# Softmax of head pairs reordered, V products ahead of scores, one K read in halves

## The chip, the cores and the metric

The kernel runs on one core of a Trainium2 chip. Its engines each run their own instruction stream in order: TensorE (PE in the profile, its weight loads PEld), VectorE (DVE), ScalarE (ACT), GpSimd (POOL) and SyncE (SP), which here only issues DMAs. The metric is the device time of one execution in microseconds (us); the median of three runs before the change is 1168.55.

## The reference

Eight tokens of width 512 go through two layers of the same shape. Each layer is grouped-query attention with a cache, and then a small dense block, each with layer norm ahead of it and a residual behind it:

```python
def _A_ref(x, k_cache, v_cache, wq, wo):
    q = (x @ wq).reshape(B, 1, 32, 128)          # 32 query heads
    k = jnp.repeat(k_cache, 4, axis=1)           # 8 K/V heads, 8192 keys each
    v = jnp.repeat(v_cache, 4, axis=1)
    p = softmax(einsum("bhqd,bhkd->bhqk", q, k) * 128 ** -0.5)
    return einsum("bhqk,bhkd->bhqd", p, v).reshape(B, 1, 4096) @ wo

x = x + _A_ref(layernorm(x), ...)
x = x + silu(layernorm(x) @ w1) @ w2
# ... and both lines once more, with the same caches and weights
```

Everything is bf16. K and V of one batch entry and one head are 2 MB each, 128 MB for each cache. Both layers read the same caches, but layer 2 of a batch entry can only begin when its layer 1 is done.

## The kernel before, in words

**Tasks.** A task is (layer, batch entry, K/V head); there are 2 x 8 x 8 = 128. The code counts layers from 0 and so does this text. `make_tasks` orders them: for each batch entry b, heads 0 to 2 of layer 0, then heads 3 to 7 of layer 0, some filling tasks of other entries, then heads 3 to 7 of layer 1, whose K is still in the memory on the chip ("kept": the last KEEP = 20 of the 32 quarters of K), and later heads 0 to 2 of layer 1, whose K is read again. V is read in both layers.

**Positions.** The main loop (L1105) walks positions p, eight for each task (GPT) and two for each quarter of a head's keys (GPG). At each position it issues, in this order: the transposes of the quarter that comes next (`emit_t_until`), the scores of the quarter just complete (`emit_s`), the product of probabilities and V of the quarter that lies LP = 22 positions back (`emit_pv`), the steps that finish a head, `emit_own`, `emit_join` and `emit_fold`, one phase of the softmax of the task two back (`softmax`, phase p % 8), a step of the dense block, the normalisation (`emit_norm`), and the reads whose place has come (`issue_until`). Since each engine takes its instructions in order, this order is the order on every engine.

**A task's work.** K lies in one of 28 slots of 512 KB (a quarter of a head each). VectorE transposes it in place (L516, 1.2 us a quarter). TensorE makes the scores: `emit_s` at L606, or, for kept heads of a pair, `score_both` at L578. Heads 4 and 5, and 6 and 7, are pairs (DUOS): their softmax is made together, with scores in two PSUM banks. The softmax has phases: 0, row maxima and a maximum over the partitions on GpSimd (L620 to L629); 2, the shift and the first exponential on ScalarE (L635 to L642, with the row sums as a by-product); 3, for a pair, the transposition of the first probabilities on TensorE (L667) and the second exponential; 4, the sums scaled by the head mask (L652 on ScalarE for a single head, L655 on VectorE for a pair) and summed over the partitions on GpSimd (L658); 5, the last transposition and the copy to PT (L674); 7, the reciprocal (L681). The probabilities, the joined output and the fold's input all share the tile E, so `emit_own` (L728, ScalarE) must wait for the transpositions, `emit_join` (L736, VectorE) for L728, and the fold (L750, TensorE) for the join. `emit_norm` (L760, VectorE) multiplies by the reciprocal. `emit_pv` (L711) takes two quarters at once for a head of a pair, at even quarters.

**Reads.** `plan_loads` lists every read with the position that needs it, sorts by that, and deals slots: a read's place (`after`) is the position behind which its slot is free, and never earlier than that of the read ahead of it. All reads go through SyncE's queue in this one order, so one read that waits for its slot holds all behind it. A V read of a single head is 512 KB, of a pair's head 1 MB (two slots). Kept K of heads 4 to 7 is read in one piece of 2 MB (READ[g] = 4, four slots); kept K of head 3 too. Slots of V come free behind L711, slots of K that is not kept behind L606 in the same layer, slots of kept K behind the scores of layer 1, which `emit_s` makes for all four quarters at the third one (SCORED = 2).

**Scores of kept heads.** In layer 0 a head whose K came in pieces of READ[g] quarters is scored when a piece's last quarter has been transposed: with READ[7] = 4, at the fourth quarter. The two lines that decide this:

```python
w = NGRAN if layer else READ[g]
if whole and (k != SCORED if layer else k % w != w - 1):
    return
```

Of the kernel before, what the change touches and what calls it, by code (L numbers as in the profile page):

```python
# [19 lines left out]
READ = (1, 1, 1, 4, 4, 4, 4, 4)  # L20
DUOS = (4, 6)
KEEP = 20
LT = 1
# [121 lines left out]
class Load:  # L145


    __slots__ = ("kind", "b", "g", "k", "turn", "need", "free", "slot", "after", "wide")

    def __init__(self, kind, b, g, k, need, free, wide=1):  # L150
        self.kind, self.b, self.g, self.k, self.turn = kind, b, g, k, k
        self.need, self.free, self.wide = need, free, wide
        self.slot, self.after = None, None
# [48 lines left out]
def plan_loads(tasks, kept, nslot, ngran):  # L202

    at = {t: i for i, t in enumerate(tasks)}
    loads = []
    for i, (layer, b, g) in enumerate(tasks):
        for k in range(ngran):
# [8 lines left out]
            w = members(g)  # L216
            if k % w == 0:
                loads.append(Load("V", b, g, k, i0 + GPG - 1 + LP, i0 + GPG - 1 + LP, w))
    loads.sort(key=lambda d: (d.need, d.kind == "K" and d.wide == 1))
# [43 lines left out]
def _build(ctx, nc, A_x, A_k_cache, A_v_cache, A_wq, A_wo, B_w1, B_w2, out):  # L263
# [43 lines left out]
    def half(slot, h):  # L307
# [30 lines left out]
              "top": DR, "tops": DR, "ssm": DR, "xn": KT // 2, "hs": FT // 2}  # L338
    widths.update({f"ssa{n}": DR for n in range(NST)})
# [71 lines left out]
    v_slot = {}  # L411

    def issue(d):
        cache = A_k_cache if d.kind == "K" else A_v_cache
        own, lead, n = d.g - lead_of(d.g), lead_of(d.g), members(d.g)
        if d.kind == "K":
            rows = cache[d.b, lead:lead + n].rearrange("g (p f) d -> (g p) (f d)", p=128 // n)
            at = own if d.wide > 1 else d.k * n + own
            src = rows[:, at * d.wide * SLOT:(at + 1) * d.wide * SLOT]
        else:  # L420
            src = cache[d.b, d.g].rearrange("(k p c) d -> k p (c d)", k=NGRAN // n, p=128)[d.k // n]
# [7 lines left out]
    with nc.Block() as block:  # L429

        @block.sync
        def _(sync_eng):
# [137 lines left out]
            def score_both(ti, slots, qn):  # L570
                own = tasks[ti][2] - lead_of(tasks[ti][2])
                cols = NGRAN // 2 * 128
                many = ARENA[:, slots[0] * SLOT:(slots[0] + NGRAN) * SLOT].rearrange(
                    "p (k u t x h j e) -> p u t h e k x j", u=2, t=NQ, x=CPB, h=PAIRS, e=2, j=QUAD)
                for u in range(2):
# [3 lines left out]
                            SCp[bank][t * QUAD:t * QUAD + USED, own * cols:(own + 1) * cols], QB[qn][:, n, :],  # L579
# [4 lines left out]
            def emit_s(i):  # L584
# [10 lines left out]
                if whole and members(g) > 1:  # L595
                    score_both(ti, slots, qn)
# [51 lines left out]
            def softmax_sum(ti):  # L648
                st, many = turn_of[ti] % NST, members(tasks[ti][2])
                w = many * REP  # L650
                if many == 1:
                    op(act, lambda: act.activation(ssm[:, 0:w], hm[:, :], ACT.Copy, scale=rs[st][:, 0:1]),  # L652
                       reads=["hm", f"rs{st}"], writes=["ssm"])
                else:
                    op(dve, lambda: dve.scalar_tensor_tensor(  # L655
                        ssm[:, 0:w], rs[st][:, 0:1].to_broadcast([128, w]), rs[st][:, 1:2], hm2, op0=ALU.add, op1=ALU.mult),
                       reads=["hm2", f"rs{st}"], writes=["ssm"])
# [43 lines left out]
            def emit_pv(i):  # L701
                ti = i // GPT
                b, g, k, _h = where(i)
                if k % members(g):
                    return
# [486 lines left out]
```

## Time and profile before

| what | value |
| --- | --- |
| runs | 1166.80, 1169.06, 1168.55 us; median 1168.55 |
| profiled execution | 1169.76 us, of which the span from the first to the last instruction is 1168.0 |
| TensorE matmul busy | 692.2 us, 59% of the span |
| VectorE busy | 738.9 us, 63% |
| ScalarE busy | 315.1 us, 27% |
| GpSimd busy | 90.7 us, 8% |
| read from HBM | 465.05 MB, mean 400 GB/s |
| mean granted TensorE clock | 0.616 |

Busy shares are means over stages with different limits. The table of windows splits the span into stretches and gives for each the busy time of every engine, the granted clock, the share of DMA time and the rate; the timeline gives single instructions with the idle time ahead of them in brackets and what ended it; the table of waits sums such idle times by pair. A share of DMA time over 1 means that packets overlap on an engine.

### The profile page before, as it was taken

How to read it: one execution, taken by the hardware profiler on the slowest of the kernel's cores; microseconds unless marked ns; L12 is line 12 of the kernel's file. 1: busy time of each engine (PE TensorE's matmuls, PEld its weight loads, DVE VectorE, ACT ScalarE, POOL GpSimd, SP SyncE). 2: the span in 40 equal slices, each digit the busy share in tenths (PEclk: the TensorE clock that was granted, in tenths of full speed). 3: DMA queues.
4: the chain of work that ended last, by engine and by line, in shares of the span. 5: the costliest groups of instructions: out<-in, count | busy, mean ns of one | idle time of the engine just before them, and what ended most of it. 6: DMA issues, size and time to landing. Idle time of an engine off the chain costs nothing.

```text
span 1168.0 us, 28238 instructions
## 1 busy us (share of the span) xinstructions
PE 692.2 (59%) x11792; PEld 377.8 (32%) x11792; DVE 738.9 (63%) x1719; ACT 315.1 (27%) x700; POOL 90.7 (8%) x232
## 2 busy tenths in 40 slices
PE   1525566556665566466665575456765576466676
PEld 1212343234233243133332342234332343133343
DVE  3836655876387664777477655777467664777473
ACT  0342123222322223312222233213322233312322
POOL 0000010001000010001100010001100010001000
PEclk9855565556655575655666577655565555666665
DMA  9999999999999999999999999999999999999993
GB/s 361 404 401 399 408 402 426 417 389 408 401 419 383 399 407 421 422 373 410 412 422 413 395 407 424 420 387 402 412 423 412 391 405 419 423 393 409 412 411 147
DMA packets 94175, 466.90 MB, mean 400 GB/s; under 512 B 9936, under 2 KB 14048, under 8 KB 71904
## 3 DMA queue, kind: packets, MB, share of 16 engines
q1 hardware_dynamic: 94048, 465.10, 98.8%
q8 instruction: 93, 1.52, 0.5%
q14 instruction: 34, 0.28, 0.1%
HBM read 465.05 MB, written 0.01 MB: 398 GB/s over the span
## 4 chain that ended last, share of the span: by engine, by line
DMA 40%; PE 19%; DVE 17%; issue 12%; ACT 6%; SPq 3%; POOL 2%; DVEq 0%; ACTq 0%; POOLq 0%
DMA arena<-in_A_k_cache_dram 33%; DMA arena<-in_A_v_cache_dram 7%; DVE E L736 6%; PE OTp L711 6%; DVE arena L516 4%; ACT E L642 4%; DVE row L620 3%; PE SCp L578 3%; SPq L394 3%; PE TPp L667 2%; PE SCp L606 2%; PE MISC L855 2%; ACT PT L674 1%; PE MISC L873 1%; PE OTp L750 1%
## 5 line engine op out<-in xcount | busy, mean ns | idle before, releaser
L516 DVE STREAM_TRANSPOSE arena<-arena 128x1024 int32<-128x1024 int32 x352 | 430.1, 1231 | 120.0 <-DMA arena<-in_A_k_cache_dram 119.9
L642 ACT ACTIVATE E<-SCp,row 128x512 bf16<-128x512 f32 x128 | 180.8, 1413 | 538.1 <-DVE row L638 463.5
L711 PE MATMUL OTp<-arena,PT 128*16 128x512 bf16 (+1 forms) x2064 | 259.9, 560 | 50.9 <-DMA arena<-in_A_v_cache_dram 31.0
L736 DVE SCALAR_TENSOR_TENSOR E<-OTp,row,E 128x128 f32<-128x128 f32 x381 | 130.4, 342 | 115.3 <-ACT E L728 97.9
L606 PE MATMUL SCp<-arena,QB 128*16 128x128 bf16 (+1 forms) x3328 | 139.3, 314 | 101.6 <-DVE arena L516 87.0
L667 PE MATMUL TPp<-ident,E 128*128 128x128 bf16 x512 | 73.4, 293 | 121.1 <-ACT E L642 120.5
L578 PE MATMUL SCp<-arena,QB 128*16 128x256 bf16 x2048 | 114.0, 389 | 47.1 <-DVE arena L516 30.4
L606 PEld LDWEIGHTS SCp<-arena,QB 128*16 128x16 bf16 x3328 | 70.3, 110 | 173.5 <-DVE arena L516 138.8
L667 PEld LDWEIGHTS TPp<-ident,E 128*128 128x128 bf16 x512 | 41.6, 125 | 185.9 <-ACT E L642 164.2
L750 PE MATMUL OTp<-row,E 128*128 128x4 f32 x254 | 66.4, 332 | 47.3 <-DVE E L736 46.9
L750 PEld LDWEIGHTS OTp<-row,E 128*128 128x128 f32 x254 | 55.4, 272 | 115.6 <-DVE E L736 103.2
L578 PEld LDWEIGHTS SCp<-arena,QB 128*16 128x16 bf16 x2048 | 61.0, 117 | 97.1 <-DVE arena L516 46.1
L629 POOL PARTITION_ALL_REDUCE row<-row x96 | 36.0, 375 | 689.7 <-DVE row L626 575.1
L728 ACT ACTIVATE E<-OTp,row 128x128 f32<-128x128 f32 x127 | 47.4, 373 | 152.4 <-PE OTp L711 152.4
L620 DVE TENSOR_REDUCE row<-SCp 128x1 f32<-128x512 f32 x128 | 86.3, 674 | 2.8
L711 PEld LDWEIGHTS OTp<-arena,PT 128*16 128x16 bf16 (+1 forms) x2064 | 53.5, 107 | 84.7 <-DMA arena<-in_A_v_cache_dram 40.4
L873 PE MATMUL MISC<-at,wo 128*128 128x32 bf16 x1024 | 37.0, 186 | 56.4 <-DVE at L760 55.3
L674 ACT COPY PT<-TPp 128x256 bf16<-128x256 bf16 x128 | 44.3, 372 | 84.6 <-PE TPp L667 84.6
L658 POOL PARTITION_ALL_REDUCE row<-row x96 | 41.3, 431 | 297.5 <-ACT row L652 137.9
L655 DVE SCALAR_TENSOR_TENSOR row<-row 128x8 f32<-128x8 f32 x32 | 7.3, 229 | 88.7 <-ACT E L642 88.7
L873 PEld LDWEIGHTS MISC<-at,wo 128*128 128x128 bf16 x1024 | 32.6, 104 | 65.9 <-DVE at L760 58.8
L563 DVE TENSOR_TENSOR QB<-QSp,row 128x64 bf16<-128x64 f32 (+1 forms) x128 | 24.0, 194 | 15.7 <-PE QSp L547 14.6
(104 smaller groups left out, 385.5 us busy)
## 6 DMA issues: line engine op xcount, KB each, us to landing
arena<-in_A_v_cache_dram SPq DMA_DIRECT2D x256, 512.0 KB, 8.5
arena<-in_A_v_cache_dram SPq DMA_DIRECT2D x128, 1024.0 KB, 12.2
arena<-in_A_k_cache_dram SPq DMA_DIRECT2D x192, 512.0 KB, 8.1
arena<-in_A_k_cache_dram SPq DMA_DIRECT2D x40, 2048.0 KB, 16.1
wq<-in_A_wq_dram SPq DMA_DIRECT2D x1, 4096.0 KB, 17.3
wo<-in_A_wo_dram SPq DMA_DIRECT2D x1, 4096.0 KB, 33.3
w<-in_B_w_dram SPq DMA_DIRECT2D x2, 1792.0 KB, 24.8
E<-in_A_x_dram SPq DMA_DIRECT2D x1, 8.0 KB
```

The source lines that it names most:

```text
L516: op(dve, lambda: dve.transpose(words, words), reads=[r_half(slot, 0), r_half(slot, 1)], writes=[r_half(slot, 0), r_half(slot, 1)])
L578: lambda n=n, t=t: pe.matmul(SCp[bank][t * QUAD:t * QUAD + USED, own * cols:(own + 1) * cols], QB[qn][:, n, :], many[:, u, t, n // 2, n % ...
L606: lambda n=n, t=t: pe.matmul(SCp[bank][t * QUAD:t * QUAD + USED, lo * 128:(lo + len(slots)) * 128], QB[qn][:, n, :], keys(t, n), start=(n ...
L620: op(dve, lambda: dve.tensor_reduce(rowmax[:, n:n + 1], SCp[bank][:, :], AX.X, ALU.max), reads=[f"SC{bank}"], writes=["rowmax"])
L642: op(act, lambda: act.activation(P[:, :].rearrange("p (x j k) -> p k x j", x=CPB, k=NGRAN), SCp[bank][:, :].rearrange("p (k x j) -> p k x ...
L667: lambda c=c: pe.transpose(tpv[:, c, :], P[:, c * 128:(c + 1) * 128], ident[:, :])
L674: op(act, lambda: act.copy(PT[pb][:, :, :, :, :].rearrange("p a t x r -> p x t a r"), tpv.rearrange("p x (t q) -> p x t q", q=QUAD)[:, :, ...
L711: lambda t=t, y=y, slot=slot, pb=pb: pe.matmul(OTp[ob][t * QUAD:t * QUAD + w * REP, 0:w * DH], PT[pb][:, at, t, y * w:(y + 1) * w].rearran ...
L728: op(act, lambda: act.activation(joint, OTp[ob][:, 0:DH], ACT.Copy, scale=own_x[:, 0:1]), reads=[f"OT{ob}", "own_x"], writes=["P"])
L736: op(dve, lambda x=x: dve.scalar_tensor_tensor(joint, OTp[ob][:, x * DH:(x + 1) * DH], own_x[:, x:x + 1], joint, op0=ALU.mult, op1=ALU.add ...
L750: lambda: pe.matmul(OTp[ob][:, 0:REP], joint, hm[:, :], start=True, stop=True)
L873: lambda o=o, h=h: pe.matmul(MISC[:, o * w:(o + 1) * w], wo_sb[:, h, o * 128:(o + 1) * 128], rhs_of(h).to_broadcast([128, w]) if n == 1 el ...
```

## The change

Six things are changed.

1. READ of head 7 goes from 4 to 2: its kept K is read in two pieces of 1 MB, and in layer 0 `score_both` is called for each half, with the columns that belong to it. In layer 1 it is still called once.
2. At positions where a kept head would be scored, `emit_pv` is issued ahead of `emit_s`.
3. For a pair, phases move: the first transposition and the second exponential from phase 3 to 4, the last transposition and the copy to PT from 5 to 6, the sums from 4 to 7. Phase 6 is issued ahead of `emit_own`, `emit_join` and `emit_fold` of the same position, all other phases behind them as before.
4. For a pair, the two row sums are scaled by the mask in two ScalarE instructions into 16 columns, in place of one on VectorE into 8; GpSimd's sum is over 16 columns; VectorE adds the two halves ahead of the reciprocal.
5. The reciprocal is made in `emit_norm` of the first head of a task or pair instead of phase 7.
6. `plan_loads` gets a loop: V reads of 1 MB with fewer than AMPLE = 8 positions between place and need are cut in two. `emit_pv` follows each read's width.

The diff, cut to its core:

```diff
-READ = (1, 1, 1, 4, 4, 4, 4, 4)
+READ = (1, 1, 1, 4, 4, 4, 4, 2)
+AMPLE = 8
...
 def plan_loads(tasks, kept, nslot, ngran):
+    apart = set()
+    while True:
+        loads = deal(tasks, kept, nslot, ngran, apart)
+        close = {d.key for d in loads if d.kind == "V" and d.wide > 1 and d.need - d.after < AMPLE}
+        if not close:
+            return loads
+        apart |= close
...
-            at = own if d.wide > 1 else d.k * n + own
+            at = (own * NGRAN + d.k) // d.wide if d.wide > 1 else d.k * n + own
...
-            def score_both(ti, slots, qn):
+            def score_both(ti, slots, qn, first):
                 own = tasks[ti][2] - lead_of(tasks[ti][2])
-                cols = NGRAN // 2 * 128
+                lo = (own * NGRAN + first) // 2 * 128
+                hi = lo + len(slots) // 2 * 128
...
             def softmax_sum(ti):
                 st, many = turn_of[ti] % NST, members(tasks[ti][2])
                 w = many * REP
-                if many == 1:
-                    op(act, lambda: act.activation(ssm[:, 0:w], hm[:, :], ACT.Copy, scale=rs[st][:, 0:1]),
-                       reads=["hm", f"rs{st}"], writes=["ssm"])
-                else:
-                    op(dve, lambda: dve.scalar_tensor_tensor(
-                        ssm[:, 0:w], rs[st][:, 0:1].to_broadcast([128, w]), rs[st][:, 1:2], hm2, op0=ALU.add, op1=ALU.mult),
-                       reads=["hm2", f"rs{st}"], writes=["ssm"])
-                op(pool, lambda: pool.partition_all_reduce(ssa[st][:, 0:w], ssm[:, 0:w], 128, bass.bass_isa.ReduceOp.add),
+                for n in range(many):
+                    op(act, lambda: act.activation(ssm[:, n * w:(n + 1) * w], masks[many][0], ACT.Copy, scale=rs[st][:, n:n + 1]),
+                       reads=["hm", "hm2", f"rs{st}"], writes=["ssm"])
+                op(pool, lambda: pool.partition_all_reduce(
+                    ssa[st][:, 0:many * w], ssm[:, 0:many * w], 128, bass.bass_isa.ReduceOp.add),
                    reads=["ssm"], writes=[f"ssa{st}"])
...
             def softmax_rcp(ti):
-                st, w = turn_of[ti] % NST, members(tasks[ti][2]) * REP
+                st, many = turn_of[ti] % NST, members(tasks[ti][2])
+                w = many * REP
+                if many > 1:
+                    op(dve, lambda: dve.tensor_tensor(ssa[st][:, 0:w], ssa[st][:, 0:w], ssa[st][:, w:2 * w], ALU.add),
+                       reads=[f"ssa{st}"], writes=[f"ssa{st}"])
                 op(dve, lambda: dve.reciprocal(ssa[st][:, 0:w], ssa[st][:, 0:w]), reads=[f"ssa{st}"], writes=[f"ssa{st}"])
...
-                elif ph == 3 and many > 1:
+                elif ph == 4 and many > 1:
                     emit_turn(ti, 0)
                     softmax_exp(ti, 1)
                 elif ph == 4:
                     softmax_sum(ti)
-                elif ph == 5:
+                elif ph == 5 and many == 1 or ph == 6 and many > 1:
                     emit_turn(ti, many - 1)
                     emit_pt(ti)
-                elif ph == 7:
-                    softmax_rcp(ti)
+                elif ph == 7 and many > 1:
+                    softmax_sum(ti)
...
             def emit_norm(ti):
                 layer, b, g = tasks[ti]
                 ob, st, own = ti % 2, turn_of[ti] % NST, g - lead_of(g)
+                if not own:
+                    softmax_rcp(ti)
...
-                if p % GPG == GPG - 1 and p < NG:
+                scored = p % GPG == GPG - 1 and p < NG
+                behind = scored and (tasks[p // GPT][2], p % GPT // GPG) in kept
+                if scored and not behind:
                     emit_s(p)
                 if (p - LP) % GPG == GPG - 1 and 0 <= p - LP < NG:
                     emit_pv(p - LP)
+                if behind:
+                    emit_s(p)
+                probs = p // GPT - 2
+                due_now = 0 <= probs < ntask and lead_of(tasks[probs][2]) == tasks[probs][2]
+                if due_now and p % GPT == 6:
+                    softmax(probs, 6)
...
-                ti = p // GPT - 2
-                if 0 <= ti < ntask and lead_of(tasks[ti][2]) == tasks[ti][2]:
-                    softmax(ti, p % GPT)
+                if due_now and p % GPT != 6:
+                    softmax(probs, p % GPT)
```

## The prediction

> **What bounds the kernel now.** First the page: its row of DMA shares and its table of queues.
>
> ```profile
> DMA  9999999999999999999999999999999999999993
> q1 hardware_dynamic: 94048, 465.10, 98.8%
> ```
>
> The transfers are busy in every slice but the last. 465 MB have to come in, the change adds no byte, and the last 19 us (from 1149) hold no pair of heads: they stay. So I ask only where the stream runs below its rate. The table of windows of 10 us, whose last columns are DMA share and GB/s, shows it:
>
> ```profile
> 480.00:490.00 10.00, 4.85 (x57) 2.32 (x56) 8.26 (x19) 2.34 (x5) 0.82 (x2) 0.68 1.01 418
> 500.00:510.00 10.00, 6.20 (x92) 3.14 (x84) 9.33 (x18) 0.37 (x1) 0.00 (x0) 0.67 1.00 376
> 510.00:520.00 10.00, 6.15 (x106) 3.54 (x106) 7.26 (x15) 3.75 (x7) 0.77 (x2) 0.50 0.93 334
> 540.00:550.00 10.00, 6.87 (x163) 4.59 (x164) 7.54 (x21) 3.38 (x12) 1.41 (x4) 0.58 1.02 408
> ```
>
> It runs at 415 to 426 where reads of 1 and 2 MB dominate, at 408 where all are 512 KB, and dips once per batch: 350 at 110, 363 at 240, 349 at 370, 334 at 510, 377 at 640, 356 at 770, 363 at 910, 381 at 1040. Against 415, with the slice beside each, that is 15.8 us in all; no gain at these places can exceed it. The dips come when head 7 of a batch has been scored. What is late there, by the waits:
>
> ```profile
> DVE row L655 <- ACT E L642: 88.7, 32, 3.7
> SPq L107 <- PE OTp L711: 431.4, 152, 7.7
> SPq L394 <- PE SCp L578: 91.0, 19, 9.3
> ```
>
> VectorE stands still 32 times, 2.8 us each, until ScalarE has made the second exponential of a pair; SyncE waits for V products (L711) to free slots. The timeline of one dip (batch 3; x in brackets is the idle time before):
>
> ```profile
> 496.57 0.23 DVE L655 SCALAR_TENSOR_TENSOR row<-row 128x8 f32<-128x8 f32 x1 [2.49 <-ACT E L642]
> 499.68 1.06 PE L711 MATMUL OTp<-arena,PT 128*16 128x512 bf16 x8
> 499.81 1.25 DVE L516 STREAM_TRANSPOSE arena<-arena 128x1024 int32<-128x1024 int32 x1 [1.86 <-DMA arena<-in_A_k_cache_dram]
> 500.84 0.33 SPq L394 DMA_DIRECT2D arena<-in_A_v_cache_dram  x1
> ...
> 506.09 1.25 DVE L516 STREAM_TRANSPOSE arena<-arena 128x1024 int32<-128x1024 int32 x1 [0.35 <-DMA arena<-in_A_k_cache_dram]
> 507.46 1.07 PE L711 MATMUL OTp<-arena,PT 128*16 128x512 bf16 x8
> 508.62 0.33 SPq L394 DMA_DIRECT2D arena<-in_A_v_cache_dram  x1
> 515.44 0.23 DVE L655 SCALAR_TENSOR_TENSOR row<-row 128x8 f32<-128x8 f32 x1 [2.64 <-ACT E L642]
> 522.29 1.25 DVE L516 STREAM_TRANSPOSE arena<-arena 128x1024 int32<-128x1024 int32 x1 [1.94 <-DMA arena<-in_A_k_cache_dram]
> ```
>
> Three L516 wait for landings, and they gauge the stream. From 499.81 (head 7's K) to 506.09 (the next K) lie 2.62 MB: 6.28 us, 417 GB/s, no gap. From 506.09 to 522.29 lie 6.29 MB (three 1 MB reads of V, six 512 KB reads of K): 16.20 us, 388 GB/s. The seven batches that show both waits have a second stretch of 15.67, 16.46, 16.20, 15.58, 15.79, 15.97 and 16.38, mean 16.01. At 416 to 424 GB/s it takes 15.1 to 14.8. So 0.9 to 1.2 us per batch is truly lost; the rest of a dip is engines that ran ahead and wait for the slowest.
>
> **The change, part by part.**
>
> *V products first.* For kept heads L711 is issued ahead of the scores at the same position: layer 0's last quarter, layer 1's third. At 498.00 the scores of head 6 (1.89 us) stood ahead of the product at 499.68; its probabilities were ready at 497.89 (end of the L674 copies), so it can start 1.8 us earlier, and the V read of 500.84 leaves at about 499.1. The product at 507.46 stood behind the scores of head 7 (505.79, which waited for transposes); its V lands about 4.9 us after head 7's K, at 504.7, so the read of 508.62 leaves near 506. These are what the stretch behind 506.09 lacks: with them 4.2 MB not yet landed at 506 are issued by 509, or 10 us of stream, to about 516, and the next V read (513.53, behind the product at 512.37, which nothing here moves) and K read (514.60) come in time. The stretch then runs at full rate: 0.9 to 1.2 us per batch.
>
> *Row sums on ScalarE, later.* L655 leaves VectorE: 32 x 0.229 = 7.3 us busy and 88.7 us of standing still. ScalarE gets 64 x 0.295 = 18.9 us (row of L652), beside 315 us in a span of 1168. The all-reduce on GpSimd is twice as wide: L658 has 0.398 to 0.519 over both widths, so nothing to 0.1 us each; the result is used ten positions later. The added addition is 32 x 0.16 (row of L623), and the reciprocal of every head moves to the normalisation, where VectorE waits for the fold (L750) anyway: 0.17 to 0.35 us beside a wait; were that cover gone, 96 such steps would be about 22 us, of which only those in the dips (some 4 per batch, 8 us) count. What is late next: the join L736 needs the copy L728, which needs the second transposition, which needs the same exponential. In the dip: exponential done 515.41, transposition 0.61, L674 0.65, L728 0.37: join at 517.0 instead of 518.00. So of the 2.64 us wait 1.0 is left, and reads behind it leave 0.6 to 1.0 earlier; this backs the term above and I count it no second time.
>
> *Phases moved by one or two positions.* The first transposition moves from phase 3 to 4, the second and L674 from 5 to 6, ahead of L728; no score or product stands between phases 3 and 4 on TensorE. In phase 7 the product follows its L674 with little between; it was ready at 497.89 before, and the chain that makes it is the same. Nothing; at worst the product waits for one more L674 copy, 0.37 us, at 2 pairs per batch: 16 x 0.37 = 6 us.
>
> *Head 7's K in two reads.* By the planner's rules 616 reads become 624; every other read keeps position and slot. The first half lands 1.05 MB or 2.5 us earlier, then V of head 4, then the second half 2.5 us later than the whole did. Transposes three and four of head 7 then run 502.3 to 504.8 instead of 503.25 to 505.73: 0.9 us, hidden, since the next K lands at 506.06 as before. Scores cost 8 x (4 groups x 0.62 - 1.88) = 4.8 us more on TensorE, beside its waits for transposes (1.01 us idle ahead of 505.79). Rows of a read are halved: were they as slow as those of the 512 KB stretch (408 against 424), 16.8 MB take 1.5 us more; if as fast, nothing. I take nothing: V's reads of that row length are part of the fast stretches.
>
> Here a rule speaks against it. The trace has 408 GB/s through 540 to 550, all 512 KB reads, or 1.28 us each: no fixed time shows between reads. The Trainium skill, "DMA: Bandwidth & Descriptors", section on the anatomy of one DMA, gives a read issued through GpSimd about 2 us fixed, besides its bytes. By that, an estimate, eight more reads would be 16 us; these reads are issued by SyncE, and the row decides.
>
> *The planner's apart rule* never fires: each double V read has 8 positions between place and need, and the limit is 8. Nothing.
>
> *Layer 1.* At the entry of layer 1 the trace has 350 GB/s at 290 to 300 (1.6 us lost), 395 at 560, elsewhere little: 3.5 us over all batches. The score of head 3 (293.63, 1.88 us) stood ahead of the product at 295.30 there. Between nothing and 3 us gained; I take nothing, nearest to most batches.
>
> **Sum.** 8 x 0.9 to 1.2 = 7.2 to 9.4; I take 8. The profiled execution was 1169.76 (span 1168.0 and 1.8 around it), so 1161.8 for it; the median of the runs shown is 1.2 below, so **1160.5**. Bounds: gains to 9.4 + 3 = 12.4, or 1156; costs of 1.5 and half of the 6 leave 1165.
>
> **Rivals.**
>
> *The gain is given back* (15%): the product at 512.37 and the K landing at 522.29 stay, because the queue's latency, not its content, sets them. For: reads issued at 508 to 514 stood 8 us to landing all the same. Then 0 to 3 us: about 1167.
>
> *The whole dips go* (7%), if engines running ahead count too: 1168.55 - 15.8 = 1153.
>
> *Products delay the scores that free K slots* (15%, slower). In layer 1 the score releases a 2 MB quad, for which SyncE waits (91.0 us in 19 waits). A single head's product (4 matmuls, 0.60 us) now stands ahead of four of five scores per batch, and if its V has not landed, the score waits with it (L711 waited 31.0 us for V, in 19 waits). It decides where under about 1 us of reads is queued. At 460 to 490 the stream holds 418 to 424 GB/s with reads that land up to 20 us after issue, so there it is covered. If the cover were gone everywhere, 32 x 0.60 = 19 us; at the entry of layer 1 alone 8 x 0.6 = 4.8 us, and with no gain elsewhere 1173.4.
>
> *Each read pays a fixed time* (2%, slower): 512 KB land in 8.5 us, 1 MB in 12.2, so 4.8 us does not scale; unhidden, 8 x 4.8 = 38 us, 1207. The 408 GB/s stretch speaks against it. The page named above states the same rule with its own figure.
>
> *It does nothing* (3%): DMA is 98.8% busy and no dip moves: 1168.5.
>
> The forecast holds the remaining 58%. About 0.2% (2.3 us) is what a measurement of this kernel can tell from no change. Faster by more: 58 + 7 + half of the 15 = 72%; within: 8 + 3 = 11%; slower: 17%. The range 1153 to 1169 leaves out the slower cases.
>
> **What would show it.** Right: no L655 wait on VectorE; about 1 us of wait at the joins of pairs instead; the second stretch near 15.0 us; dips above 390 GB/s; V reads leaving about 2 us earlier after head 7's K lands. Wrong: dips unchanged in depth, the second stretch still 16 us, new waits of L578 or L606 in layer 1 behind products, SyncE's wait for L578 above 91 us, or reads of 1 MB that take the stream below 415 at 480 to 500.

## The result and the profile after

| what | before | after |
| --- | --- | --- |
| median (20 runs each, side by side) | 1168.53 us (1165.43 to 1171.03) | 1171.24 us (1168.36 to 1175.75) |
| ratio, 95% interval | 1 | 1.0025 [1.0014, 1.0036] |
| span of the profiled execution | 1168.0 us | 1171.1 us |
| VectorE busy | 738.9 us | 749.8 us |
| ScalarE busy | 315.1 us | 331.4 us |

The change is slower by 2.7 us; the forecast was faster by 8. The page of the changed kernel, its row of DMA shares and its queue:

```profile
DMA  9999999999999999999999999999999999999993
q1 hardware_dynamic: 95200, 465.10, 98.6%
```

The stream is still busy everywhere and moves the same bytes. The windows of 10 us (columns: us; busy and count of PE, PEld, DVE, ACT, POOL; granted clock; DMA share; GB/s):

```profile
500.00:510.00 10.00, 6.66 (x135) 4.02 (x124) 7.88 (x15) 0.37 (x1) 0.37 (x1) 0.66 1.02 410
510.00:520.00 10.00, 7.10 (x138) 4.38 (x138) 6.98 (x15) 4.26 (x9) 0.47 (x1) 0.52 0.90 351
520.00:530.00 10.00, 4.52 (x78) 1.59 (x66) 5.15 (x8) 0.37 (x1) 0.00 (x0) 0.50 1.02 399
530.00:540.00 10.00, 5.89 (x103) 3.33 (x103) 8.39 (x18) 2.41 (x5) 1.19 (x3) 0.50 1.01 390
540.00:550.00 10.00, 7.80 (x173) 5.11 (x174) 7.32 (x20) 3.39 (x12) 1.24 (x3) 0.50 1.02 402
```

The dip did not go, it spread. The slice at 500 rises from 376 to 410, as hoped, and that at 510 only from 334 to 351; but 520 to 550, which had 412, 408 and 408, now has 399, 390 and 402. From 490 to 550 the six rates add up to 2375 instead of 2361 (423 at 490 in both): 0.14 MB in 60 us, or 0.3 us, no gain that can be told. The waits (who waited for whom; us in total, times, longest):

```profile
DVE arena L533 <- DMA arena<-in_A_k_cache_dram: 155.1, 98, 19.5
DVE E L755 <- ACT E L747: 140.9, 55, 6.3
...
SPq L108 <- PE OTp L730: 374.6, 159, 7.0
SPq L408 <- PE SCp L596: 110.9, 26, 8.9
```

The 88.7 us of VectorE at the pair's sums are gone from this table. What VectorE no longer waits there it waits at the join (L755 is the old L736: 97.9 before) and at landings of K (L533 is the old L516: 119.9 before): 43.0 + 35.2 = 78 us of the 88.7 are back in those two rows. (The fastest version below has 133.4 and 166.2 us in the same rows, so this move of the wait is not by itself what makes a kernel slower.) SyncE waits 57 us less for V products (L730) and 20 us more for scores (L596). The timeline of the same dip:

```profile
498.13 1.03 PE L730 MATMUL OTp<-arena,PT 128*16 128x512 bf16 x8 [0.78 <-issue]
...
499.25 0.33 SPq L408 DMA_DIRECT2D arena<-in_A_v_cache_dram  x1
...
505.18 1.25 DVE L533 STREAM_TRANSPOSE arena<-arena 128x1024 int32<-128x1024 int32 x1 [1.18 <-DMA arena<-in_A_k_cache_dram]
505.19 0.33 SPq L408 DMA_DIRECT2D arena<-in_A_v_cache_dram  x1
...
510.35 0.13 DVE L698 TENSOR_TENSOR row<-row 128x8 f32<-128x8 f32 x1
510.51 0.20 DVE L700 RECIPROCAL row<-row 128x8 f32<-128x8 f32 x1
510.82 0.16 DVE L781 TENSOR_TENSOR at<-OTp,row 128x4 bf16<-128x4 f32 x1
510.90 0.16 DVE L653 SCALAR_TENSOR_TENSOR row<-row 128x8 f32<-128x8 f32 x1
...
511.34 1.46 ACT L660 ACTIVATE E<-SCp,row 128x512 bf16<-128x512 f32 x1 [7.71 <-DVE row L656]
...
513.15 0.33 SPq L408 DMA_DIRECT2D arena<-in_A_v_cache_dram  x1
...
522.26 1.25 DVE L533 STREAM_TRANSPOSE arena<-arena 128x1024 int32<-128x1024 int32 x1 [3.22 <-DMA arena<-in_A_k_cache_dram]
```

The V reads leave at 499.25 and 505.19 instead of 500.84 and 508.62: that part of the forecast happened. But the head's chain on VectorE now has the addition and the reciprocal (510.35 to 510.71) right ahead of the normalisation (L781) and the shift (L653); the exponential begins at 511.34 (511.75 before), the V read that leaves next, at 513.15 (513.53 before). Counted from the landing of K that opens the stretch (505.18 here, 506.09 before) the exponential is 0.5 us later than before (6.16 against 5.66) and that V read as well (7.97 against 7.44), and the stretch up to the next landing (522.26) takes 17.1 us instead of 16.2.

### The profile page after: what moved, and what is told of

The parts are those of the page before. It is cut to its first block, busy times and chain, and to the rows that moved or that the text cites. A ratio compares the mean times of both kernels' runs of the same rounds, so it can differ in the third digit from the quotient of the medians.

```text
span 1171.1 us, 28880 instructions
## 1 busy us (share of the span) xinstructions
PE 689.3 (59%) x12048; PEld 383.1 (33%) x12048; DVE 749.8 (64%) x1719; ACT 331.4 (28%) x764; POOL 92.8 (8%) x232
## 4 chain that ended last, share of the span: by engine, by line
DMA 45%; PE 17%; DVE 15%; issue 11%; ACT 6%; SPq 3%; POOL 2%; DVEq 0%; ACTq 0%; POOLq 0%
DMA arena<-in_A_k_cache_dram 39%; DMA arena<-in_A_v_cache_dram 7%; DVE E L755 6%; PE OTp L730 5%; ACT E L660 3%; DVE arena L533 3%; PE SCp L596 3%; SPq L408 3%; DVE row L638 3%; PE TPp L682 3%; ACT PT L689 2%; PE SCp L624 2%; PE OTp L769 2%; PE MISC L894 2%; PE MISC L876 1%
## 5 line engine op out<-in xcount | busy, mean ns | idle before, releaser
L533 DVE STREAM_TRANSPOSE arena<-arena 128x1024 int32<-128x1024 int32 x352 | 432.3, 1235 | 155.6 <-DMA arena<-in_A_k_cache_dram 155.1
L730 PE MATMUL OTp<-arena,PT 128*16 128x512 bf16 (+1 forms) x2064 | 253.0, 554 | 76.2 <-DMA arena<-in_A_v_cache_dram 35.8
L755 DVE SCALAR_TENSOR_TENSOR E<-OTp,row,E 128x128 f32<-128x128 f32 x381 | 131.1, 344 | 150.2 <-ACT E L747 140.9
L624 PE MATMUL SCp<-arena,QB 128*16 128x128 bf16 (+1 forms) x3328 | 136.6, 309 | 92.5 <-DVE arena L533 77.8
L596 PE MATMUL SCp<-arena,QB 128*16 128x256 bf16 (+1 forms) x2304 | 114.3, 363 | 20.3 <-ACT E L660 13.3
L624 PEld LDWEIGHTS SCp<-arena,QB 128*16 128x16 bf16 x3328 | 70.7, 109 | 162.2 <-DVE arena L533 121.7
L596 PEld LDWEIGHTS SCp<-arena,QB 128*16 128x16 bf16 x2304 | 72.1, 121 | 73.2 <-issue 38.7
L638 DVE TENSOR_REDUCE row<-SCp 128x1 f32<-128x512 f32 x128 | 87.4, 683 | 3.3
L730 PEld LDWEIGHTS OTp<-arena,PT 128*16 128x16 bf16 (+1 forms) x2064 | 46.8, 99 | 115.7 <-issue 62.8
L670 ACT ACTIVATE row<-row 128x4 f32<-128x4 f32 (+1 forms) x128 | 38.6, 301 | 2.7
L660 ACT ACTIVATION_READ_ACCUMULATOR E<-SCp,row 128x1 f32 x128 | 34.0, 266 | 0.0
```

Source lines behind the costliest of these rows:

```text
L533: op(dve, lambda: dve.transpose(words, words), reads=[r_half(slot, 0), r_half(slot, 1)], writes=[r_half(slot, 0), r_half(slot, 1)])
L596: lambda n=n, t=t: pe.matmul(SCp[bank][t * QUAD:t * QUAD + USED, lo:hi], QB[qn][:, n, :], many[:, u, t, n // 2, n % 2], start=(n == 0), st ...
L624: lambda n=n, t=t: pe.matmul(SCp[bank][t * QUAD:t * QUAD + USED, lo * 128:(lo + len(slots)) * 128], QB[qn][:, n, :], keys(t, n), start=(n ...
L638: op(dve, lambda: dve.tensor_reduce(rowmax[:, n:n + 1], SCp[bank][:, :], AX.X, ALU.max), reads=[f"SC{bank}"], writes=["rowmax"])
L660: op(act, lambda: act.activation(P[:, :].rearrange("p (x j k) -> p k x j", x=CPB, k=NGRAN), SCp[bank][:, :].rearrange("p (k x j) -> p k x ...
L730: lambda t=t, y=y, slot=slot, pb=pb: pe.matmul(OTp[ob][t * QUAD:t * QUAD + w * REP, 0:w * DH], PT[pb][:, at, t, y * w:(y + 1) * w].rearran ...
```

## The experiments

Each ran beside the kernel before on the same chip, though not all on one chip; ratios are to it, with 95% intervals. "Early reciprocal" is used below for one that isn't issued in the normalisation.

**The parts of the change, undone or alone.** First the changed kernel without the halves of head 7:

```diff
-READ = (1, 1, 1, 4, 4, 4, 4, 2)
+READ = (1, 1, 1, 4, 4, 4, 4, 4)
```

> The changed kernel with head 7's K again read in one piece of 2 MB; everything else as changed. Theory A (the two halves cost it: shorter rows in 16.8 MB of reads, 1.5 to 3 us, and nothing else of the change matters to the stream): back to the time of the kernel before, within 1 us. Theory B (the halves are harmless, and the moved phases or the order of products and scores put in a new wait): stays 2 to 3 us slower than before, or is slower still, because the first half no longer lands early. Theory C (each part gains or loses by itself and they cancel): 3 us or more faster than before.

Measured: 1168.57, ratio 1.0000 [0.9988, 1.0013]. Without the halves the loss is gone, and no gain is left either. This run alone does not say whether the other parts do nothing, or gain and lose and cancel; the next ones do.

The kernel before with READ[7] = 2 and what that needs in `score_both`:

> The kernel before with one part of the change alone: head 7's K read and scored in two halves. Theory A: 1.5 to 3 us slower than before. Theory B: within 1 us of before, or up to 1 us faster, since the transposes of head 7 end 0.9 us earlier. Theory C: cannot be told from A by this one alone.

Measured: 1169.65, 1.0010 [0.9997, 1.0023].

The kernel before with V products ahead of scores at kept heads, nothing else:

```diff
-                if p % GPG == GPG - 1 and p < NG:
+                if scored and not behind:
                     emit_s(p)
...
+                if behind:
+                    emit_s(p)
```

> The kernel before with V products ahead of the scores of kept heads, and nothing else changed. My prediction's mechanism: 4 to 8 us faster, since V slots come free about 2 us earlier in each dip. Theory A (the dips are engines waiting for the slowest, and cost no time): within 1 us. Theory B in the form of the rival (products delay the scores that free K slots): 2 to 5 us slower.

Measured: 1167.94, 0.9989 [0.9976, 1.0002]. The term forecast at 8 us gave 1.3, and perhaps nothing. In its profiled execution the second stretch, from one landing of K to the next, takes 15.64 us in the mean of the same seven batches, where the kernel before has 16.01: 0.4 us less and not 0.9 to 1.2. (The extra reciprocal at phase 7 below, whose time cannot be told from that of the kernel before, has 15.89, so a tenth or two is chance.)

The kernel before with the softmax part alone (moved phases, sums on ScalarE, addition and reciprocal in the normalisation):

> The kernel before with the softmax part alone: phases moved, sums on ScalarE, the addition and the reciprocal in the normalisation. Prediction: 0 to 5 us faster, VectorE's wait of 88.7 us gone. Theory A: within 1 us, the wait shows up at the join and at the landings of K in its place. Theory B in its other form (the reciprocal and the addition stand ahead of the normalisation, the join waits for L728): 2 to 3 us slower.

Measured: 1172.83, 1.0046 [1.0029, 1.0063]. The loss is here, in the part that was costed at nothing.

The same without the moved phases (sums on ScalarE in phase 4, addition and reciprocal in the normalisation):

> The kernel before with the sums of pairs on ScalarE and the addition and reciprocal in the normalisation, phases where they were (exponential 3, sums 4, copy 5). If the softmax part is slow because VectorE no longer waits at L655 (it runs ahead and something else is then out of step), this is 3 to 5 us slower too. If it is slow because the copy to PT comes one position later, this is within 1 us of before or faster.

Measured: 1174.95, 1.0053 [1.0037, 1.0070]. So the moved phases cost nothing measurable; the loss is in the sums or in the reciprocal.

**The stream by itself.** All reads in their order, with no compute behind the first layer norm (it leaves out everything else of both layers); and the same with head 7's K in halves:

> Leaves out all work after the first layer norm: no transposes, scores, softmax, products or dense block. All reads of the kernel before are issued in the same order, size and slots, and each waits only for the read that used the slot before it; then a tile of zeros is written out. It gauges what the stream takes with the queue always full. Theory A (the dips cost no time, the stream itself is the bound): 1135 to 1150 us, as the kernel before has its last byte at about 1149. Theory B (the stream is held up by slots that come free late): 1095 to 1125 us, which is 465 MB at 415 to 425 GB/s.

> As the stream alone (the same work left out), but with the reads of the changed kernel: head 7's K in two halves, 624 reads for 616. If the shape of the halves costs the stream, it is 1.5 to 3 us above the stream alone; if not, equal within 0.5 us, and what the halves cost in the whole kernel comes from when they land.

Measured: 1131.01, 0.9675 [0.9653, 0.9696], and 1131.43, 0.9675 [0.9650, 0.9700]. The rates of the first, in 40 equal slices of its span:

```profile
GB/s 358 410 396 422 412 410 425 423 415 410 417 423 419 412 410 422 423 417 411 413 425 420 414 410 424 423 414 411 410 425 422 416 409 418 423 419 412 411 416 311
```

Behind the first three slices and ahead of the last none is under 409. A dip is thus made by the engines and not by the shape of the reads. Of the 1168.8 - 1131.0 = 38 us by which the kernel is longer, not all are lost to reads that leave late. By the windows of 10 us the reads end near 1149 in the kernel before (372 GB/s from 1140 to 1150, then 7) and near 1122 here (409 from 1110, then 94 from 1120), an estimate that gives late reads some 27 us; the rest is work behind the last read. Eight more reads cost the stream 0.4 us, within the spread of its runs (1130.88 to 1132.21). The Trainium skill's "DMA: Bandwidth & Descriptors", section on the anatomy of one DMA, which states a fixed time for each read that a GpSimd issue makes, would have made them 16 us by the estimate in the prediction; for reads issued by SyncE into a full queue this run speaks against using it.

The kernel before without the 352 transposes L516 (the scores are then of K as it lies):

> The kernel before without any transposition of K (L516 left out, so that the scores are of K as it lies). VectorE loses 430 us of its 739 and no score waits for it. Theory A: within 3 us of before, since the stream sets the time. Theory B (slots come free late because VectorE is late): 15 us or more faster, up to the stream alone plus the tail of 19 us.

Measured: 1153.78, 0.9868 [0.9846, 0.9890]. VectorE is then busy for 351 us instead of 739, and the gain is 15 us. The reads now end near 1136 (240 GB/s from 1130 to 1140), so some 13 of the 27 us that late reads cost hang on the transposes, on VectorE itself or in the scores that wait for them.

**The reciprocal alone.** The kernel before with one instruction moved, 96 times:

```diff
-                elif ph == 7:
-                    softmax_rcp(ti)
...
             def emit_norm(ti):
+                if not own:
+                    softmax_rcp(ti)
```

> The kernel before with one edit: the reciprocal leaves phase 7 and is made in the normalisation of the first head of a task. Theory L (the reciprocal now stands on VectorE between a fold that is already done and the next shift, so the first exponential and all reads behind it leave 0.2 to 0.5 us later in every dip): 3 to 5 us slower. Theory V (it is the missing wait at L655 that does harm: VectorE runs ahead and the transposes fall at other times): within 1 us of before.

Measured: 1174.81 to 1168.12, 1.0055 [1.0036, 1.0075]. This single move costs 6.4 us, all that the softmax part costs. First the place in the kernel before, then in this one (timelines, batch 3):

```profile
509.96 0.23 DVE L626 SCALAR_TENSOR_TENSOR row<-row 128x8 f32<-128x8 f32 x1
510.10 1.24 DVE L516 STREAM_TRANSPOSE arena<-arena 128x1024 int32<-128x1024 int32 x1
...
511.26 0.12 DVE L760 TENSOR_TENSOR at<-OTp,row 128x4 bf16<-128x4 f32 x1
511.31 0.15 DVE L635 SCALAR_TENSOR_TENSOR row<-row 128x8 f32<-128x8 f32 x1
...
511.44 0.60 PE L873 MATMUL MISC<-at,wo 128*128 128x32 bf16 x16 [1.97 <-DVE at L760]
...
512.37 1.06 PE L711 MATMUL OTp<-arena,PT 128*16 128x512 bf16 x8
...
513.53 0.33 SPq L394 DMA_DIRECT2D arena<-in_A_v_cache_dram  x1
```

```profile
510.57 0.23 DVE L626 SCALAR_TENSOR_TENSOR row<-row 128x8 f32<-128x8 f32 x1
510.71 1.24 DVE L516 STREAM_TRANSPOSE arena<-arena 128x1024 int32<-128x1024 int32 x1
...
511.87 0.16 DVE L681 RECIPROCAL row<-row 128x8 f32<-128x8 f32 x1
512.14 0.16 DVE L760 TENSOR_TENSOR at<-OTp,row 128x4 bf16<-128x4 f32 x1
512.22 0.16 DVE L635 SCALAR_TENSOR_TENSOR row<-row 128x8 f32<-128x8 f32 x1
...
512.36 0.61 PE L873 MATMUL MISC<-at,wo 128*128 128x32 bf16 x16 [2.04 <-DVE at L760]
...
513.29 1.06 PE L709 MATMUL OTp<-arena,PT 128*16 128x512 bf16 x8
...
514.45 0.33 SPq L394 DMA_DIRECT2D arena<-in_A_v_cache_dram  x1
```

From L626 to the normalisation L760 it was 1.30 us and is 1.57. VectorE does not wait there for another engine: the transpose ends and the next instruction follows at once, L760 before and the reciprocal here. TensorE does wait there, for L760 (L873, the output projection), and gets it 0.31 us later. The product of V that is queued behind on TensorE (L711, here L709) and the V read that leaves next are 0.31 us later as well, counted from L626 (2.72 instead of 2.41, and 3.88 instead of 3.57): at this place the whole delay reaches a read. TensorE has no idle time between L873 and that product in either, so to this read it is the normalisation that carries it. The exponential begins 0.30 us later, too (2.09 instead of 1.79), and feeds what comes after.

**The sums with an early reciprocal.** First the kernel before with the pair's sums still on VectorE, but issued at phase 6 instead of 4, two positions further behind the second exponential; then sums on ScalarE, with addition and reciprocal at phase 7; then the latter with V products first:

```diff
-                elif ph == 4:
+                elif ph == 4 and many == 1 or ph == 6 and many > 1:
                     softmax_sum(ti)
```

> The kernel before with one edit: the sum of a pair stays on VectorE (L655) but is issued at phase 6 instead of 4, when the second exponential is done, so that VectorE waits there little or not at all. Reciprocal at phase 7 as before. Prediction's mechanism: 3 to 8 us faster. Theory L: within 1 us of before, as the wait moves to the landing of K and the join. Theory V: 3 to 5 us slower.

Measured: 1166.00, 0.9981 [0.9966, 0.9996]. VectorE's wait there does not go away by this; it falls from 88.7 to 58.4 us.

> The sums-alone kernel (1.0053 of before) with the addition and the reciprocal put back to phase 7; sums still on ScalarE and 16 columns on GpSimd. Theory L: back to the time of before, within 1.5 us. Theory V, or a cost of the wider sum on GpSimd or of ScalarE's two instructions: stays 4 to 6 us slower.

Measured: 1167.15, 0.9986 [0.9969, 1.0002]. With addition and reciprocal back at phase 7 the loss of 0.0053 is gone, so it lay there and not in the sums on ScalarE.

> The best of the parts: V products first, sums on ScalarE, addition and reciprocal at phase 7, phases and the 2 MB read as before. Theory L: 1 to 4 us faster than before. Theory V: within 1 us of before, as the kernel without halves was.

Measured: 1162.39 (1161.55 to 1164.65), 0.9951 [0.9931, 0.9971]: faster than both kernels. The windows of its dip:

```profile
490.00:500.00 10.00, 5.11 (x55) 2.67 (x56) 6.54 (x15) 4.31 (x9) 0.47 (x1) 0.50 1.00 418
500.00:510.00 10.00, 7.20 (x125) 3.89 (x126) 9.57 (x18) 1.80 (x3) 0.37 (x1) 0.67 1.00 396
510.00:520.00 10.00, 5.45 (x118) 2.93 (x119) 5.52 (x12) 3.17 (x8) 0.46 (x1) 0.67 0.98 381
520.00:530.00 10.00, 5.17 (x99) 2.40 (x88) 6.87 (x14) 1.62 (x3) 0.38 (x1) 0.50 1.01 408
530.00:540.00 10.00, 5.58 (x123) 3.14 (x120) 7.03 (x15) 2.77 (x9) 1.37 (x4) 0.67 1.03 410
```

The slices from 490 to 530 had 423, 376, 334 and 412, in sum 1545, and have 418, 396, 381 and 408, in sum 1603: 0.58 MB more in 40 us, or 1.4 us. One dip in one execution can't show that this is the gain, though: the extra reciprocal at phase 7 below, as fast as the kernel before, fills the two slices nearly as far,

```profile
500.00:510.00 10.00, 6.48 (x126) 3.54 (x118) 8.08 (x16) 2.08 (x4) 0.37 (x1) 0.73 0.99 385
510.00:520.00 10.00, 6.16 (x126) 3.46 (x118) 7.41 (x14) 2.42 (x6) 0.40 (x1) 0.50 1.00 378
```

and the late reciprocal, which loses, has 398 and 342. What counts is the ratio. V products first and sums off VectorE are worth 5.7 us once nothing is put into the normalisation. Apart they gave 1.3 and 1.6; that they give more together lies within the intervals. This version was measured on one chip, and the two that build on it below on others.

**Where the late reciprocal costs it.** Behind the reciprocal stand the normalisation, which feeds the output projection on TensorE, and the shift, which feeds the exponential. First the kernel before with an extra reciprocal of a scratch tile right ahead of the shift, and with the same one at phase 7:

```diff
                 elif ph == 2:
+                    op(dve, lambda: dve.reciprocal(tiny["dum"][:, 0:many * REP], tiny["dum"][:, 0:many * REP]), reads=["dum"], writes=["dum"])
                     softmax_shift(ti)
```

> The kernel before with one extra reciprocal of a scratch tile (0.17 us, read by nobody) on VectorE in phase 2, right ahead of the shift. Theory L1 (the late reciprocal costs because the shift, its exponential and the transposes behind it come later): slower as with the late reciprocal, 1.004 to 1.007. Theory L2 (it costs because the normalised sums reach the output projection on TensorE later): the normalisation is not delayed here, so no more than 1.001. Theory L3 (any VectorE time of that size costs): slower as with L1, and the twin at phase 7 as well.

> The kernel before with the same extra reciprocal at phase 7, behind the real one, where the next instruction of the chain on VectorE is three phases away. Theory L1 and Theory L2: 0.999 to 1.001, since nothing of the chain stands behind it. Theory L3: 1.004 to 1.007, as in the twin ahead of the shift.

Measured: 1169.97, 1.0013 [0.9998, 1.0027], and 1168.54, 1.0004 [0.9991, 1.0017]. Another 14 to 16 us of VectorE time, by itself, cost nothing that shows. But the first test was weaker than planned:

```profile
508.52 0.12 DVE L762 TENSOR_TENSOR at<-OTp,row 128x4 bf16<-128x4 f32 x1
508.56 0.19 DVE L689 RECIPROCAL row<-row 128x8 f32<-128x8 f32 x1
508.67 0.12 DVE L636 SCALAR_TENSOR_TENSOR row<-row 128x8 f32<-128x8 f32 x1
```

Nothing reads the scratch tile, so the shift starts 0.11 us behind its start; the median delay of the shift is 0.06 us. The next two swap the order instead: the shift is issued ahead of the normalisation, in the kernel before and in the fastest version.

```diff
-                elif ph == 2:
+                elif ph == 1:
                     softmax_shift(ti)
+                elif ph == 2:
                     softmax_exp(ti, 0)
```

> The kernel before with the shift of the scores (two VectorE instructions, 0.15 and 0.16 us) issued one position earlier, so that VectorE does it right ahead of the normalisation and no more right behind it; 96 times. The shift then ends about 0.15 us earlier, the normalisation about 0.35 us later. Theory L1 (the late shift, and the exponential behind it, carries the cost of the late reciprocal, about 0.4 us of the whole for each us of delay): faster, 0.993 to 0.998. Theory L2 (the late normalisation, for which TensorE waits with the output projection, carries it): slower, 1.003 to 1.010. Both equally: 0.999 to 1.003.

> The version with sums on ScalarE, early reciprocal and V products ahead of scores (0.9951 of the kernel before) and, added to it, the same swap of shift and normalisation on VectorE. Theory L1: 0.989 to 0.993 of the kernel before. Theory L2: 0.998 to 1.004. Both equally: 0.994 to 0.997.

Measured: 1171.77, 1.0040 [1.0026, 1.0055], and 1166.59, 0.9998 [0.9984, 1.0013], the latter 0.0047 above the version without the swap. The place in the first of them:

```profile
511.28 0.12 DVE L635 SCALAR_TENSOR_TENSOR row<-row 128x8 f32<-128x8 f32 x1
511.44 0.16 DVE L638 TENSOR_REDUCE row<-row 128x1 f32<-128x8 f32 x1
511.51 0.15 DVE L761 TENSOR_TENSOR at<-OTp,row 128x4 bf16<-128x4 f32 x1
511.69 1.43 ACT L642 ACTIVATE E<-SCp,row 128x512 bf16<-128x512 f32 x1 [6.29 <-DVE at L761]
...
511.73 0.57 PE L874 MATMUL MISC<-at,wo 128*128 128x32 bf16 x16 [2.22 <-DVE at L761]
```

The bracket of the exponential names the last VectorE event ahead of it; it starts 0.09 us behind the end of the shift (511.60), as it did before (0.10).

The mean times from the start of L626 (the shift by its second instruction, L638), each from the timeline of one profiled execution (96 steps; 94 for the normalisation; 26 for the output projection, those within 4 us), as differences from the kernel before (us):

| kernel | normalisation | shift | exponential | output projection | ratio |
| --- | --- | --- | --- | --- | --- |
| before | 0.995 | 1.393 | 1.651 | 1.511 | 1 |
| late reciprocal | +0.22 | +0.16 | +0.16 | +0.24 | 1.0055 |
| extra one ahead of the shift | -0.01 | +0.04 | +0.04 | -0.01 | 1.0013 |
| extra one at phase 7 | -0.01 | -0.01 | -0.01 | -0.03 | 1.0004 |
| shift ahead | +0.41 | -0.09 | -0.07 | +0.27 | 1.0040 |
| changed kernel | +0.30 | +0.24 | +0.24 | +0.35 | 1.0025 |
| fastest version | -0.01 | -0.01 | -0.01 | -0.03 | 0.9951 |

With the swap the shift and the exponential come earlier and only the normalisation and what waits for it come later, and the kernel loses 4.7 us, in the fastest version 0.0047 or 5.5. So the late normalisation alone makes a loss of that size; the theory that the late exponential carries all of it (which expected a gain here) falls. How the two share the 6.4 us of the late reciprocal is not shown: scaled by the delay of the output projection (0.24 against 0.27 us) the normalisation would account for some 4 us of them, by its own delay (0.22 against 0.41) for 2.5, both estimates.

**The changed kernel with an early reciprocal; and halves again.** The changed kernel, with addition and reciprocal issued six positions ahead of the normalisation:

```diff
-                if not own:
-                    softmax_rcp(ti)
...
+                if p % GPT == 3 and 0 <= probs - 1 < ntask and lead_of(tasks[probs - 1][2]) == tasks[probs - 1][2]:
+                    softmax_rcp(probs - 1)
```

> The changed kernel with the addition of the two halves of the sums and the reciprocal taken out of the normalisation and issued at phase 3 of the task before the normalisation's, six positions ahead of it; all else as changed. Theory L (the late reciprocal is what the change loses): 1.0025 less 0.0055, so 0.995 to 0.998 of the kernel before. Rival H (the halves and the moved phases lose on their own): 0.999 to 1.003.

Measured: 1164.38, 0.9969 [0.9955, 0.9984]. With that one step undone the change is a gain of 3.6 us.

The fastest version, with READ[7] = 2 added:

> The version with sums on ScalarE, early reciprocal and V products ahead of scores (0.9951 of the kernel before) and, added to it, the last kept quad read in halves. If the halves cost what the run that took them out of the changed kernel showed, 0.9951 plus 0.0025, so 0.997 to 0.998; if they cost nothing, as in the run with reads alone, 0.9945 to 0.996.

Measured: 1165.98, 0.9983 [0.9966, 1.0001]. So halves gain nothing, and may cost. Three pairs measure them: 1.0010 alone, 1.0025 to 1.0000 in the changed kernel, 0.9983 to 0.9951 here, that is 0.1 to 0.3%. The first lies within its interval, the intervals of the second pair just part, and those of the third overlap. All three have the same sign; by what way is open, since the reads as such cost nothing that shows.

## Why the prediction was wrong

The parts add up. Fastest version -0.0049, late reciprocal +0.0055, halves +0.0010 to +0.0032: +0.0016 to +0.0038, and the change measured +0.0025. In microseconds: of the 8 forecast, 5.7 are there in the fastest version, the late reciprocal takes 6.4 and the halves 1 to 4. Gain and late reciprocal about cancel, as the changed kernel without halves shows (1.0000).

**The step that failed** is the cost of the moved reciprocal, put as: "the reciprocal of every head moves to the normalisation, where VectorE waits for the fold (L750) anyway". In layer 0 it hardly waits there. The rows that say so are in the profile of before, and the step did not read them (columns: busy, mean ns of one; idle ahead of it):

```profile
L760 DVE TENSOR_TENSOR QT<-OTp,row 128x4 bf16<-128x4 f32 x64 | 9.0, 141 | 14.0 <-PE OTp L750 10.9 <-PE OTp L744 3.1
L760 DVE TENSOR_TENSOR at<-OTp,row 128x4 bf16<-128x4 f32 x64 | 8.5, 133 | 1.4 <-PE OTp L750 1.4
```

In layer 0 (the row that writes `at`) there are 1.4 us of idle time for 64 normalisations, 0.02 us each, and what is needed to cover one step is 0.27. In layer 1 (`QT`) there are 14.0 us, 0.22 each in the mean, but in 15 waits only. The sentence behind it gave the price without cover as 8 us, and the single move measured 6.4 [4.2, 8.8]. The zero was chosen on a cover that was assumed. That the price came near may be luck: it counts four steps of each batch, those in the dips, and no run shows that only those cost.

**V products first, 8 us:** the reads leave earlier as worked out, by 1.6 and 3.4 us in the profiled execution, and 0.7 and 2.5 us earlier counted from the K that opens the stretch. What was mis-sized is the step from there to the time, "the stretch then runs at full rate: 0.9 to 1.2 us per batch": with V products first alone it got 0.4 us shorter. Alone the move gave 1.3 us [-0.2, 2.8]; with the sums off VectorE and an early reciprocal the two gave 5.7 us [3.4, 8.1]. The gauge was poor: the second stretch was to fall from 16.01 to 15.0; its mean is 16.88 in the changed kernel, which is slower, but 15.88 in the fastest version, which gains 5.7 us. It takes the starts of transposes for landings, which holds only where they wait; in the fastest version the first of the two waits 0.2 us or less in six of the seven batches. *Layer 1,* 0 to 3 us: the slice at 290 did fill, from 350 to 406 GB/s, but those from 250 to 280 fell from 412, 409 and 409 to 387, 386 and 386 in the changed kernel (one execution each).

**The pair's sums, "I count it no second time":** issued two positions later, on VectorE, they alone gave 2.2 us [0.5, 4.0], with a third of the wait gone. What is late next was named rightly for the join (43.0 us more over 32 pairs, 1.3 each, for the 1 us named); with the landings of K it took up 78 of the 88.7 us.

**Moved phases, nothing:** right (1.0046 with, 1.0053 without). The 6 us of the worst case didn't come.

**Halves, nothing to 1.5 us:** for the stream by itself right, 0.4 us in the run with reads alone. In the kernel they cost 1 to 4 us, by a way that isn't shown.

**The apart rule:** right. The changed kernel has the same 128 reads of 1 MB of V.

**Rivals.** "The gain is given back" comes nearest for V products first alone, with its 0 to 3 us. Its sign, that the K landing at 522.29 stays, did come (522.26), but says little: that landing is at 517.20 with the extra reciprocal at phase 7, whose time is that of the kernel before. And the rival had no loss in it. "Products delay the scores" was the rival for a slower kernel; SyncE does wait 20 us more for scores, but the same order of products is in the fastest version, where that wait is 110.2 us as well. The true slower case, a step added ahead of what another engine waits for, was in the text only as a remark on a cover, without a chance of its own. Of the signs of being wrong, the second stretch and SyncE's wait for scores (110.9 us) came.

What stays open is how the late normalisation spreads: TensorE's output projection starts 0.24 to 0.27 us later behind it, and in the place shown the product and the V read behind it too, but no run took the projection away by itself. The sums of TensorE's waits do not settle it: they are 56.4 us for L873 before, 60.4 with the late reciprocal, and 63.4 in the fastest version, which gains.

## What to carry to other kernels

A small instruction is covered where its engine is seen to be idle at that very place: read the idle time of the row it is put in front of, per instruction, before it is called covered. Without cover it was free only where nothing waited for what stands behind it: at phase 7 VectorE has no idle time ahead of the reciprocal (0.0 us in its row), and a second one there cost nothing that shows. When an engine works in order, ask who waits for the instruction behind the new one, also on other engines; and issue what has all its inputs (here the reciprocal, ready many positions earlier) in a place with slack. Where a change has a part that gains and a part that loses, its total says little of either, and the parts are worth running apart before the whole is dropped.

## What the runs showed of the hardware

- An instruction on VectorE that reads what the one ahead of it wrote starts later than the busy time tells: the reciprocal of 0.16 us delays the normalisation that reads it by 0.27 us from start to start (511.87 to 512.14), while an unrelated one of 0.19 us delays its follower by 0.11 (508.56 to 508.67). The Trainium skill, "Perfetto Trace Analysis", section on the lifecycle of an instruction, says that an instruction's semaphore is only pushed at its reported end, when its write is acknowledged, while the next one may begin to fetch before that; both pairs of numbers agree.
- With reads alone, a queue that never waits for compute, 465 MB came in 1129 us, 412 GB/s, and no slice between the first three and the last was under 409; the kernel before has 398 GB/s over its span and is 38 us longer.
- VectorE's busy time falls by 388 us without the transposes, and that is worth 15 us; reciprocals of 15 us in all, moved to the wrong place, cost 6.
